# A Strassen-style GEGLU feed-forward kernel: two bf16 products moved ahead, one weight load in halves, the last output tile copied by two engines

## The chip, the cores and the metric

The kernel runs on one core of a Trainium2 chip. The metric is the device time of one execution in microseconds (us), the median of several runs. The engines of a core work side by side, each on its own queue in order: TensorE (PE; its weight loads are shown as PEld), VectorE (DVE), ScalarE (ACT), GpSimd (POOL) and SyncE (SP), which issues most of the DMAs here. They wait for one another through semaphores.

## The reference

```python
def setup_inputs():
    B, S, D, F = 32, 32, 1024, 3584
    return {
        "x": _w((lambda *s: _rng.normal(s) * 0.05)(B, S, D)),
        "w_gate": _w((lambda *s: _rng.normal(s) * 0.05)(D, F)),
        "w_up": _w((lambda *s: _rng.normal(s) * 0.05)(D, F)),
        "w_down": _w((lambda *s: _rng.normal(s) * 0.05)(F, D)),
    }

def reference(x, w_gate, w_up, w_down):
    return (_gelu(x @ w_gate) * (x @ w_up)) @ w_down
```

All tensors are bf16, gelu is the tanh form. x has 1024 rows (32 x 32) of 1024.

## The kernel before

Both matrix stages are done with seven block products instead of eight (the Winograd form of Strassen's scheme). Stage 1 treats [w_gate; w_up], cut along D, as a 2 by 2 block matrix for each block i of 128 columns of F (28 blocks, FT): A11 and A12 are the two halves of w_gate along D, A21 and A22 those of w_up. x, transposed, is the other 2 by 2 matrix: B11 and B21 are its first 512 rows (xt0), B12 and B22 its last 512 rows (xt1). A product P1 to P7 of one block is four matmuls of 128x128 by 128x512 into one PSUM tile.

- P1 (`first_products`, A11 B11) and P2 (`second_products`, A12 B21, on top of P1) read the bf16 weights and bf16 x themselves: "the bf16 products". They need nothing but their weights. ACT copies P1 to e1 (L212) and takes the gelu of P1 + P2 (L219).
- P6 (`sixth_products`, S2 T2), P7 (`seventh_products`, S3 T3), P5 (`fifth_product`, S1 T1), P4 (`fourth_product`, C22 T4) and P3 (`third_product`, S4 B22) work on fp32r sums and are f32r matmuls. T1 to T4 are sums of the four quarters of x, made once by DVE (`t_sum`, L166). S1 to S4 are sums of weight blocks for each i, made by DVE or POOL (L175, L176, L180, L184); C22 and the fp32r copy of B22 are made by ACT (L187, L291).
- P6 starts from e1 in PSUM (`seed`, L225). ACT copies P6's result to e2 (L241) before P7 goes on top of it; ACT copies P7's result to e3 (L256), and DVE adds it to P5 (u, L258), before P4 goes on top of it. DVE multiplies P4's result by the gelu (L245) into gT. P3 goes on top of P5, DVE adds e2 (h, L263; one buffer), ACT takes the gelu (L265), DVE multiplies by u (L268) into gT.

The order is written out by hand (`manual_schedule`): each engine's instructions stand in the order of the Python code. First come ten warm-up matmuls, then P1 and P2 of blocks 0 to 9 alone (LEAD = 10), while x's second half and the weights arrive and DVE makes the sums. Then P5, P6, P7, P4 and P3 of blocks 0 and 1 are done together, with the bf16 products of blocks 10 and 11 in between: P1 of block 10 after P5, P1 of block 11 after P6, P2 of block 10 after P7. From block 2 on a loop does one block a turn: P6, P4 of the block before, P5, then (`ahead`, not in the turns of ALONE) P1 of block `done` and P2 of block `done` - 1, then P7 and P3 of the block before. `done` starts at 12, so P2 of block 11 stands in the turn of block 2, behind P1 of block 12. Block 2 has no block before it in this sense, so its turn has no P4 and no P3.

SP's queue issues the weights in the order written: x's first two quarters, w_gate's tiles 0 to 3 (256 columns each, some in two halves along D), half of w_up's first tile, gate tile 4, the transposing load of xt1 (L155), gate tile 5 (blocks 10 and 11; it lies in the part of gT that is written last), the other half of w_up's first tile, gate tile 6, and so on. Each waits for the landing of an earlier DMA that used its semaphore, eight of which take turns.

Stage 2 multiplies gT by w_down in the same manner (L394). The last product, for each of four tiles of 128 rows, adds fourteen f32r matmuls to X[t]; ACT copies the 128x512 result to bf16 (L506) and it is stored, the first three by SP's queue, the last by ACT's.

PSUM has four tiles with the tag p (X and some of P1 + P2) and four with q (Y, the rest of P1 + P2), used in turn.

Of the kernel before, what the change touches and what calls it, by code (L numbers as in the profile page):

```python
# [7 lines left out]
ACT = mybir.ActivationFunctionType  # L8
# [4 lines left out]
def kernel(  # L13
# [18 lines left out]
    nc = tc.nc  # L32
# [10 lines left out]
    DT = D // P  # L43
    KH = DT // 2
    FT = F // P
    NT = N // P
    DB = 512
# [3 lines left out]
    LEAD = 10  # L51
    ALONE = (4, 7, 10, 13, 16, 19, 22, 25)
    KF = FT // 2
    TT = NT // 2
# [28 lines left out]
    def load_gate(c, queue, lo=0, hi=DT):  # L83
        if c not in WG:
            WG[c] = gw.tile([P, DT, 2 * P], bf16, name="gw", tag="gw")
        queue.dma_start(
            out=WG[c][:, lo:hi, :], in_=wg_r[:, lo:hi, 2 * c * P : (2 * c + 2) * P]
        )

    def load_up(c, lo=0, hi=4):  # L90
        if c not in WU:
            WU[c] = uw.tile([P, DT, 4 * P], bf16, name="uw", tag="uw")
        nc.sync.dma_start(
            out=WU[c][:, :, lo * P : hi * P],
            in_=wu_r[:, :, (4 * c + lo) * P : (4 * c + hi) * P],
        )
# [4 lines left out]
    def a11(i):  # L101
        return block(WG, 2, i, 0)

    def a12(i):
        return block(WG, 2, i, 1)
# [18 lines left out]
    def psum_p(name):  # L124
        return psum.tile([P, NB], fp32, name=name, tag="p")

    def psum_q(name):
        return psum.tile([P, NB], fp32, name=name, tag="q")

    with tc.manual_schedule():  # L130
# [22 lines left out]
        load_gate(3, nc.sync, KH, DT)  # L153
        load_gate(4, nc.sync)
        nc.sync.dma_start_transpose(out=xt1, in_=xf[NB:N, :])  # L155
        load_gate(5, nc.sync)
        load_up(0, 2, 4)

        T = {}
# [13 lines left out]
        def early_sums(i, engine=nc.gpsimd):  # L173
            S1[i], S3[i] = weight_tile("s1"), weight_tile("s3")
            engine.tensor_tensor(S1[i], a21(i), a22(i), ALU.add)  # L175
            engine.tensor_tensor(S3[i], a11(i), a21(i), ALU.subtract)  # L176
# [14 lines left out]
        def pair_product(ps, lhs, rhs, first, cuts):  # L191
            for lo, hi in zip(cuts, cuts[1:]):
                for p, l in zip(ps, lhs):
                    for k in range(lo, hi):
                        nc.tensor.matmul(  # L195
                            p,
                            lhsT=l[:, k, :],
                            rhs=rhs[:, k, :],
                            start=(first and k == 0),
                            stop=(k == KH - 1),  # L200
                            skip_group_check=True,
                        )

        def first_products(*blocks, cuts=(0, KH)):
            for i in blocks:
                A[i] = psum_p("a") if 4 <= i < 8 else psum_q("a")
            pair_product([A[i] for i in blocks], [a11(i) for i in blocks], B11, True, cuts)
            for i in blocks:
                if i % 2 == 0:
                    pool, tag = (xpool, "e1") if i == LEAD - 2 else (ring, "ring")  # L210
                    E1[i // 2] = pool.tile([P, 2, NB], fp32, name="e1", tag=tag)
                nc.scalar.activation(E1[i // 2][:, i % 2, :], A[i], ACT.Copy)  # L212

        def second_products(*blocks, cuts=(0, KH)):
            pair_product([A[i] for i in blocks], [a12(i) for i in blocks], B21, False, cuts)
            for i in blocks:
                if i % 2 == 0:
                    GL[i // 2] = half.tile([P, 2, NB], bf16, name="gl0", tag="half")
                nc.scalar.activation(GL[i // 2][:, i % 2, :], A[i], ACT.Gelu_apprx_tanh)  # L219

        X, Y, E2, U1, G1 = {}, {}, {}, {}, {}
# [5 lines left out]
        done = LEAD + 2  # L227

        def ahead():
            nonlocal done  # L230
            if done < FT:
                first_products(done)
            second_products(done - 1)
            done += 1

        def sixth_products(*blocks):
            cuts = range(0, KH + 1, 2)
            pair_product([X[i] for i in blocks], [S2[i] for i in blocks], T["T2"], False, cuts)
            for i in blocks:
                E2[i] = epool.tile([P, NB], fp32, name="e2", tag="e2")  # L240
                nc.scalar.activation(E2[i], X[i], ACT.Copy)  # L241
# [9 lines left out]
        def seventh_products(*blocks):  # L251
            cuts = range(0, KH + 1, 2)
            pair_product([X[i] for i in blocks], [S3[i] for i in blocks], T["T3"], False, cuts)
            for i in blocks:
                e3 = epool.tile([P, NB], fp32, name="e3", tag="e3")
                nc.scalar.activation(e3, X[i], ACT.Copy)  # L256
                U1[i] = epool.tile([P, NB], bf16, name="u1", tag="u1")
                nc.vector.tensor_tensor(U1[i], Y[i], e3, ALU.add)  # L258
# [28 lines left out]
        copy_a22(0)  # L287
        second_products(8)
        second_products(9)
        for k in range(KH):  # L290
            nc.scalar.activation(T["B22"][:, k, :], B22[:, k, :], ACT.Copy)  # L291
        copy_a22(1)
# [2 lines left out]
        pair_product(  # L295
            [Y[0], Y[1]], [S1[0], S1[1]], T["T1"], True, range(KH + 1)
        )
        first_products(LEAD)
        sixth_products(0, 1)
        first_products(LEAD + 1)  # L300
        seventh_products(0, 1)
        second_products(LEAD)
        early_sums(2, nc.vector)
        second_sum(2)
        seed(2)
# [12 lines left out]
        for i in range(2, FT + 1):  # L318
# [16 lines left out]
            if here and i not in ALONE and done <= FT:  # L335
                ahead()
# [55 lines left out]
        def step(ps, lhs, rhs, j, t, first=False, last=False):  # L392
            for i in range(2):
                nc.tensor.matmul(  # L394
                    ps,
                    lhsT=lhs[:, i, t * P : (t + 1) * P],
                    rhs=rhs[:, i, :],
                    start=(first and j == 0 and i == 0),
                    stop=(last and j == JF - 1 and i == 1),
                    skip_group_check=True,  # L400
                )
# [9 lines left out]
        X = [psum.tile([P, DB], fp32, name="x", tag="p") for t in range(TT)]  # L411
# [90 lines left out]
        for t in range(TT):  # L502
            for j in range(JF):
                step(X[t], SC[j], TC[j], j, t, last=True)
            o_sb = opool.tile([P, DB], bf16, name="o_sb", tag="o")
            nc.scalar.activation(o_sb, X[t], ACT.Copy)  # L506
            queue = nc.sync if t < TT - 1 else nc.scalar
            queue.dma_start(out=of[(TT + t) * P : (TT + t + 1) * P, 0:DB], in_=o_sb)

# [29 lines left out]
```

## Time and profile before

| what | value |
| --- | --- |
| runs of the kernel | 276.03 us median of 3 (275.87 to 276.15) |
| profiled execution | 276.09 us, span 274.28 us (first to last instruction) |
| granted TensorE clock | 1.000 over the span |
| first real matmul, last matmul's end | 5.74 us, 270.97 us |
| PE busy | 268.9 us, 98% of the span |
| DVE, ACT, POOL busy | 188.6, 138.2, 87.2 us |
| DMA | 26.42 MB, mean 96 GB/s |
| matmul of 128x512: bf16, f32r (start to start in a chain) | 0.22 us, 0.23 us |

The span is what the instructions cover; the time of an execution has some 1.8 us around it. In the chain of waits a row is a piece of the chain that ended last: its start, its length, the engine and the line, how many instructions. In a timeline a row is one or more instructions of an engine in order of time, with their start, duration, line, operation, shape, and in brackets the idle time before them and what ended it. A matmul's duration there (0.38 to 0.39 us) overlaps the next one's.

### The profile page before, as it was taken

The numbers are of one execution on the slowest core, as the hardware profiler recorded it, in microseconds if no ns is written. First come the engines' busy times: TensorE is split into PE (matmuls) and PEld (weight loads), VectorE is DVE, ScalarE is ACT, GpSimd is POOL, SyncE is SP. The second block draws the span as 40 slices with busy tenths as digits, with TensorE's granted clock in tenths as the row PEclk, the third lists the DMA queues.
The fourth block names the chain that finished last, engine by engine and source line by source line (L and its number), as shares of the span: only waits on it lengthen the run. The fifth ranks groups of instructions, "written<-read, shape, count | busy, mean of one in ns | idle before, by whom it ended". The sixth has DMA issues, their size and how long they took to land.

```text
span 274.3 us, 3336 instructions
## 1 busy us (share of the span) xinstructions
PE 268.9 (98%) x1172; PEld 189.3 (69%) x1186; DVE 188.6 (69%) x226; ACT 138.2 (50%) x239; POOL 87.2 (32%) x81
## 2 busy tenths in 40 slices
PE   8999999999999999999999999999999999999995
PEld 2445667768777687776877768764447888888883
DVE  0068974866658666686666866769994999999900
ACT  2678565566556665566655666531100072860311
POOL 0000083845558455584555845600000000000000
PEclk9999999999999999999999999999999999999999
DMA  8999402153400034215360202459602000000221
GB/s 174 280 272 269 155 1 76 51 181 103 128 2 0 0 102 131 76 44 187 97 211 0 76 2 77 114 190 327 215 0 76 2 0 0 1 2 0 97 96 38
DMA packets 41008, 26.42 MB, mean 96 GB/s; under 512 B 9248, under 2 KB 40992, under 8 KB 40992
## 3 DMA queue, kind: packets, MB, share of 16 engines
q1 hardware_dynamic: 39248, 25.30, 31.8%
q10 hardware_dynamic: 1744, 0.92, 1.3%
q8 instruction: 9, 0.15, 0.2%
q14 instruction: 7, 0.06, 0.1%
HBM read 22.02 MB, written 2.10 MB: 88 GB/s over the span
## 4 chain that ended last, share of the span: by engine, by line
PE 96%; DMA 2%; issue 0%; ACT 0%
PE x L195 19%; PE x L394 18%; PE y L115 18%; PE a L195 18%; PE x L115 9%; PE y L394 9%; PE z L394 4%; DMA xt<-in_x_dram 2%; PE y L195 1%; ACT o_sb L506 0%
## 5 line engine op out<-in xcount | busy, mean ns | idle before, releaser
L195 PE MATMUL x<-T,s 128*128 128x512 f32 x224 | 63.4, 407 | 0.0
L195 PEld LDWEIGHTS x<-T,s 128*128 128x128 f32 x224 | 41.6, 188 | 10.9 <-ACT e L241 0.3
L195 PE MATMUL a<-xt,gw 128*128 128x512 bf16 x182 | 44.0, 380 | 1.1 <-DMA xt<-in_x_dram 0.5
L184 POOL TENSOR_TENSOR s<-gw,s 128x512 fp32r<-128x512 bf16 x22 | 26.0, 1184 | 48.4 <-PE y L115 47.7
L258 DVE TENSOR_TENSOR u<-y,e 128x512 bf16<-128x512 f32 x28 | 19.3, 691 | 32.0 <-ACT e L256 31.2
L180 DVE TENSOR_TENSOR s<-s,gw 128x512 fp32r<-128x512 f32 x24 | 34.4, 1434 | 0.0
L195 PEld LDWEIGHTS <-gw 128*128 128x128 bf16 x192 | 17.4, 98 | 24.4 <-issue 5.7
L265 ACT ACTIVATE gl<-h 128x512 bf16<-128x512 bf16 x28 | 17.7, 631 | 28.5 <-DVE h L263 28.5
L245 DVE TENSOR_TENSOR gT<-gl,x 128x512 bf16<-128x512 bf16 x28 | 19.2, 687 | 17.9 <-PE x L115 17.9
L115 PE MATMUL x<-T,c 128*128 128x512 f32 x112 | 30.4, 393 | 0.0
L115 PE MATMUL y<-B,s 128*128 128x512 f32 x112 | 30.2, 391 | 0.0
L175 POOL TENSOR_TENSOR s<-uw 128x512 fp32r<-128x512 bf16 x25 | 29.2, 1167 | 0.0
L115 PE MATMUL y<-T,s 128*128 128x512 f32 x104 | 27.8, 389 | 0.0
L394 PE MATMUL x<-tc,sc 128*128 128x512 f32 x112 | 25.7, 389 | 0.0
L212 ACT ACTIVATE e<-a 128x512 f32<-128x512 f32 x28 | 16.6, 597 | 17.2 <-PE a L195 17.2
L256 ACT ACTIVATE e<-x 128x512 f32<-128x512 f32 x28 | 16.7, 600 | 15.7 <-PE x L195 15.7
L176 POOL TENSOR_TENSOR s<-gw,uw 128x512 fp32r<-128x512 bf16 x21 | 24.5, 1166 | 0.0
L115 PEld LDWEIGHTS x<-T,c 128*128 128x128 f32 x112 | 20.9, 188 | 5.1 <-ACT e L256 0.7
L115 PEld LDWEIGHTS y<-B,s 128*128 128x128 f32 x112 | 21.0, 188 | 4.7
L394 PEld LDWEIGHTS x<-tc,sc 128*128 128x128 f32 x112 | 21.0, 188 | 4.4
L115 PEld LDWEIGHTS y<-T,s 128*128 128x128 f32 x104 | 19.5, 188 | 4.1
L394 PEld LDWEIGHTS <-gT 128*128 128x128 bf16 x112 | 10.9, 98 | 13.3 <-issue 0.3
(57 smaller groups left out, 346.9 us busy)
## 6 DMA issues: line engine op xcount, KB each, us to landing
uw<-in_w_up_dram SPq DMA_DIRECT2D x6, 1024.0 KB, 6.3
gw<-in_w_gate_dram SPq DMA_DIRECT2D x8, 512.0 KB, 3.9
v<-in_w_down_dram SPq DMA_DIRECT2D x5, 512.0 KB, 3.5
v<-in_w_down_dram SPq DMA_DIRECT2D x4, 640.0 KB, 8.2
v<-in_w_down_dram SPq DMA_DIRECT2D x8, 256.0 KB, 4.2
out_dram<-o_sb SPq DMA_DIRECT2D x15, 128.0 KB, 1.7
gw<-in_w_gate_dram SPq DMA_DIRECT2D x5, 256.0 KB, 3.9
uw<-in_w_up_dram SPq DMA_DIRECT2D x2, 512.0 KB, 5.7
```

The source lines that it names most:

```text
L115: nc.tensor.matmul(ps, lhsT=lhs[:, k, :], rhs=rhs[:, k, :], start=(first and k == 0), stop=(k == KH - 1), skip_group_check=True,)
L175: engine.tensor_tensor(S1[i], a21(i), a22(i), ALU.add)
L176: engine.tensor_tensor(S3[i], a11(i), a21(i), ALU.subtract)
L180: nc.vector.tensor_tensor(S2[i], S1[i], a11(i), ALU.subtract)
L184: engine.tensor_tensor(S4[i], a12(i), S2[i], ALU.subtract)
L195: nc.tensor.matmul(p, lhsT=l[:, k, :], rhs=rhs[:, k, :], start=(first and k == 0), stop=(k == KH - 1), skip_group_check=True,)
L212: nc.scalar.activation(E1[i // 2][:, i % 2, :], A[i], ACT.Copy)
L245: nc.vector.tensor_tensor(gT[:, i, 0:NB], GL[i // 2][:, i % 2, :], X[i], ALU.mult)
L256: nc.scalar.activation(e3, X[i], ACT.Copy)
L258: nc.vector.tensor_tensor(U1[i], Y[i], e3, ALU.add)
L265: nc.scalar.activation(G1[i], h1, ACT.Gelu_apprx_tanh)
L394: nc.tensor.matmul(ps, lhsT=lhs[:, i, t * P : (t + 1) * P], rhs=rhs[:, i, :], start=(first and j == 0 and i == 0), stop=(last and j == JF ...
```

## The change

In stage 1, P1 of block 10 goes in front of P5 of blocks 0 and 1 (on ACT, its copy to e1 in front of the copies of B22). P1 of block 11 takes its old place after P5, P2 of block 10 stands after P6, and P2 of block 11 after P7, in front of P4 of block 0; the loop's first `ahead` (turn of block 2) then does P1 of block 12 alone. w_gate's sixth tile (number 5, blocks 10 and 11) is loaded in two halves along D, so that P1 waits for the first half alone: one more DMA on SP's queue. At the end, ACT copies the left 256 columns of the last output tile and DVE the right 256.

```diff
-        load_gate(5, nc.sync)
+        load_gate(5, nc.sync, 0, KH)
+        load_gate(5, nc.sync, KH, DT)
         load_up(0, 2, 4)
...
             nonlocal done
             if done < FT:
                 first_products(done)
-            second_products(done - 1)
+            if done > LEAD + 2:
+                second_products(done - 1)
             done += 1
...
         second_products(8)
         second_products(9)
+        first_products(LEAD)
         for k in range(KH):
             nc.scalar.activation(T["B22"][:, k, :], B22[:, k, :], ACT.Copy)
         copy_a22(1)
...
         pair_product(
             [Y[0], Y[1]], [S1[0], S1[1]], T["T1"], True, range(KH + 1)
         )
-        first_products(LEAD)
+        first_products(LEAD + 1)
         sixth_products(0, 1)
-        first_products(LEAD + 1)
+        second_products(LEAD)
         seventh_products(0, 1)
-        second_products(LEAD)
+        second_products(LEAD + 1)
         early_sums(2, nc.vector)
...
             o_sb = opool.tile([P, DB], bf16, name="o_sb", tag="o")
-            nc.scalar.activation(o_sb, X[t], ACT.Copy)
+            part = DB if t < TT - 1 else DB // 2
+            nc.scalar.activation(o_sb[:, :part], X[t][:, :part], ACT.Copy)
+            if part < DB:
+                nc.vector.tensor_copy(o_sb[:, part:], X[t][:, part:])
```

## The prediction

> **What bounds the kernel now.** I read the page's busy shares first, then the chain of work that ended last inside the stretch that the change touches, then the timelines of ScalarE (ACT) and VectorE (DVE) there, the DMA view of the moved load, and the timeline of the end. TensorE (PE) is busy for nearly the whole span, so only PE's gaps and the two ends can give time.
>
> ```profile
> PE 268.9 (98%) x1172; PEld 189.3 (69%) x1186; DVE 188.6 (69%) x226; ACT 138.2 (50%) x239; POOL 87.2 (32%) x81
> ```
>
> The chain between 22 and 46 us (start, length, what; counted at the ends of the matmuls):
>
> ```profile
> 23.34 2.12 PE y L195 x8
> 25.45 0.23 PE a L195
> 25.69 0.05 issue
> 25.74 0.59 PE a L195 x2
> 26.34 1.85 PE x L195 x8
> 28.19 0.88 PE a L195 x4
> 29.07 1.85 PE x L195 x8
> 30.92 0.88 PE a L195 x4
> 31.80 0.93 PE x L115 x4
> ...
> 39.02 1.86 PE x L195 x8
> 40.89 0.01 issue
> 40.90 1.19 PE x L115 x4
> ```
>
> Eight f32r matmuls take 1.85 us (0.92 for one product of four), four bf16 ones 0.87 to 0.88. P5 of blocks 0 and 1 (first line) takes 2.12: it waits 0.27 for T1, which DVE makes piece by piece. P4 of block 2 (last line) takes 1.19: it waits 0.27 for ACT's copy of P7's result. So some 0.55 us of PE time is lost in this stretch; after 43 us the chain shows f32r products of 0.91 to 0.93 and no gap worth having.
>
> ACT and then DVE between 30 and 38 us:
>
> ```profile
> 30.49 1.08 ACT L256 ACTIVATE e<-x 128x512 f32<-128x512 f32 x2 [0.78 <-PE x L195]
> 35.72 0.63 ACT L265 ACTIVATE gl<-h 128x512 bf16<-128x512 bf16 x1 [2.79 <-DVE h L263]
> 37.11 0.63 ACT L265 ACTIVATE gl<-h 128x512 bf16<-128x512 bf16 x1 [0.76 <-DVE h L263]
> 37.64 0.61 ACT L187 ACTIVATE c<-uw 128x512 fp32r<-128x512 bf16 x1
> 38.16 0.58 ACT L241 ACTIVATE e<-x 128x512 f32<-128x512 f32 x1
> ```
>
> ```profile
> 29.13 2.35 DVE L166 TENSOR_TENSOR T<-xt,T 128x1024 fp32r<-128x1024 bf16 x2
> 31.40 0.68 DVE L258 TENSOR_TENSOR u<-y,e 128x512 bf16<-128x512 f32 x1
> ```
>
> A second chain runs beside PE. DVE ends T4, does u, u, the three sums of block 2, gT, h with no idle time (h of block 0 starts at 35.00), ACT's gelu follows h at 35.72, h of block 1 needs that gelu's end (one h buffer), ACT does the second gelu, the copy L187 and at 38.16 e2 of block 2, and only its end (38.74) lets P7 of block 2 start at 38.79 (P7 and the next P6 take 1.86 instead of 1.85). So this second chain has no slack against PE. It starts at DVE's u of block 0 (31.40), which T4 holds now; e3, its other input, was ready at 30.49 + 0.60 = 31.09.
>
> **The change, part by part.** PE does the same matmuls; only the order moves.
>
> *1. P1 of block 10 in front of P5.* It needs the first half of w_gate's sixth tile. The DMA view from 20.1 to 24.1 us, in slices of 0.1 us:
>
> ```profile
> GB/s 289 292 287 292 292 289 289 292 292 289 289 289 289 279 129 56 72 56 31 108 195 261 307 307 297 317 287 348 338 364 343 348 338 358 343 333 348 338 364 317
> ...
> gT<-in_w_gate_dram SPq DMA_DIRECT2D x1, 512.0 KB, 4.4
> ```
>
> SP issues the load at 20.10, right behind the transpose of x (its issue holds SP's queue from 13.38 to 20.05), and it lands 4.4 us later, 24.47. The transpose's packets fill the rate until about 21.5; summing the slices from there, 262 KB have passed at 22.85 and 524 KB at 23.61. The whole tile's landing came 0.86 after its last bytes. If the half pays that lag in full it lands at 23.71; if half of it, at 23.28; I take 23.6, near the full lag, since that is the one lag measured here. PE is free for P1 at 23.34 (matmul ends), which needs a landing by 23.13: from the landing to the end of four bf16 matmuls is 0.04 (the first landing of x, 0.74 + 4.96 = 5.70, to the first matmul at 5.74) plus 1.05 (25.30 to 26.34 now). So P1 ends at 23.6 + 1.09 = 24.69 instead of a free 24.21, PE waits 0.48, and P5, with T1 whole by then, ends at 26.54. Before, both were done at 26.34. ACT now has block 10's e1 copy in front of the four copies of B22 (from 23.87 now) and waits there until P1's end; they end some 1.4 later, near 27.4, and P3 of block 0 reads them after 33. Bounds: a landing by 23.13 makes this part 0.28 better than before, one at 23.75 some 0.35 worse.
> The Trainium skill, "DMA: Bandwidth & Descriptors", in the section Anatomy of one DMA, says that most of a DMA's fixed cost is the receipt of the last write, so it does not shrink with the size; by that rule the half pays the whole lag and part 2 would come to +0.61, by half a lag to +0.18. The 0.86 us here is such a lag.
>
> *The split's other cost* is one more issue on SP: 0.56 us (four of 256 KB in a row took 2.23 from 7.74), so the second half, block 0's up half and the next gate tile start about 0.5 later. Their covers: P2 of block 10 reads the second half near 29.3 us, DVE's S1 of block 2 the up half after 32, P1 of block 12 the gate tile (21.43 + 7.6 = 29.0 now) after 37. So it costs nothing, and 0.5 us at most without that cover. Later loads keep their distance in the queue.
>
> *2. P2 of block 10 in front of P7, P2 of block 11 in front of P4.* By PE alone: 26.54, P1 of block 11 (0.87), P6 (1.85), P2 of block 10 (0.87), so P7 starts at 30.13, against 29.07. That is 1.06 later, and T2, T3, T4 are ready at each step. But e3 of block 0 now ends at 31.09 + 1.06 = 32.15 and DVE's u starts at 32.19 instead of 31.40, 0.79 later. PE's own work in front of P4 (P2 of block 11) does not help u, it only follows P7. Everything down the second chain is back to back or waits for the step before it, so e2 of block 2 ends 0.79 later as well and P7 of block 2 starts at 38.79 + 0.79 = 39.58, while PE is done with what stands before it at 39.20: 30.13 + 1.85 for P7 + 0.87 for P2 of block 11 = 32.85, plus 3.67 for the P4 and P3 of two blocks, 1.81 for P6 and P5 of block 2, 0.87 for P1 of block 12 (P2 of block 11 has left this place). From that start P7 and the next P6 take 2.10 (38.79 to 40.89), so P4 of block 2 can start at 41.68 instead of 39.20 + 1.85 = 41.05. Behind u on DVE stand the sums of block 2, then on POOL those of block 3: S2 of block 2 ends near 35.3 for P6 at 36.5, S2 of block 3 (37.32 + 1.66 now) near 39.8 for P6 at 40.8. ACT, rid of the gelu L219 between, has e3 at 40.76 + 0.60 + 0.04 = 41.40, so the old 0.27 wait goes. Before, P4 ended at 42.09, so its free start would be 42.09 - 0.92 = 41.17: **+0.51**. In general it is landing minus 23.09, with a floor of +0.04 when the half comes in time: the gap at P5 and the one at P4 are both closed, and the sum reappears in front of P7. Behind it the chain is all PE, and I carry +0.51 to the end.
>
> *3. The last tile by two engines.* Timeline of the end:
>
> ```profile
> 271.00 0.60 ACT L506 ACTIVATE o_sb<-x 128x512 bf16<-128x512 f32 x1 [2.58 <-PE x L394]
> 271.62 0.37 ACTq L508 DMA_DIRECT2D out_dram<-o_sb  x1
> ```
>
> In the built order the DVE half does not wait for PE but for ACT's counter at the value that ACT's half raises: the halves follow each other. ACT's half: 0.60 for 512 columns less 256 of them at 0.84 ns ((1052 - 620) / 512, lines L484 and L291) = 0.38. DVE's half has no row; the nearest is DVE's sum from PSUM of 512 columns, 0.69 (L408), less 256 at 1.04 ns ((1219 - 687) / 512, L166) = 0.42; the low bound is half of the fastest DVE row of 512 columns (0.41, L268) = 0.20. With 0.03 for the step between engines: 0.38 + 0.03 + 0.42 - 0.60 = **+0.23** (from +0.01). The store then waits for DVE instead of ACT, at the same price.
> The Trainium skill, "PSUM — Partial Sum Buffer", section PSUM bank collisions raise a hardware error, says that two engines may not access one bank at the same time, and that the compiler's scheduler orders such pairs, ACT and DVE reads too. A row of 512 fp32 is one bank of 2 KiB by that page, and the built order agrees. By the rule +0.23; with both halves at once 0.42 - 0.60 = -0.18.
>
> **Sum**: 0.51 + 0.23 = +0.74. The profiled execution (276.09 us, span 274.28) would become 276.83, its span 275.02; from the median of the runs, 276.03, it is **276.8**.
>
> **Rivals.** *Cover without a price*: the half lands by 23.13 and something on the second chain gives way (DVE does the sums of block 2 before u, or e2 is not what holds P7), so PE runs free: P1 and P5 end at 23.34 + 0.87 + 1.85 = 26.06, 0.28 sooner than now, P7 of block 2 starts at 39.02 - 0.28 = 38.74 and P4 at 40.59, 0.58 better than 41.17. With the tail's +0.23 it is 275.7. For it: both old gaps lie where the products go. Against: P7's wait at 38.79 already ends with L241, and u cannot precede e3. It decides if e2 ends before 38.7. If the tail's halves also ran together (-0.18): 275.3, faster.
> *The half in time, the chain as I read it*: +0.04 + 0.23 = 276.3. For it: rates up to 364 GB/s in the second half of the transfer. Against: the 0.86 lag.
> *A late half*: packets of both halves mixed, or the lag grown, landing at 24.1: +1.0 + 0.23 = 277.3. For it: three loads wait behind the transpose. Against: the whole tile landed before the load issued after it.
> *The halves together* with the rest as forecast: +0.51 - 0.18 = 276.36. Against: the counter that DVE waits for.
>
> **How the numbers follow.** Forecast 0.52; half in time 0.18; late half 0.13; cover without a price 0.09 (a third of it with the tail together); halves together 0.08. A measurement here tells some 0.2% (0.55 us) from no change. The forecast's own spread is 0.18 to 0.61 for the moves and 0.01 to 0.23 for the tail, so about a sixth of it (0.08) stays under 0.55. Slower: the rest of the forecast and the late half, 0.57; faster: the third of the free case, 0.03; within 0.2%: 0.40. Forecast alone: 276.4 to 277.0. The range 275.9 to 277.2 leaves out half of the late case and the free case, 0.16.
>
> **What would show it.** The chain has P5 at about 1.85, some 0.5 us of DMA wait ahead of the first P1 matmul on the tile in gT, and P7 of block 2 released by L241 near 39.6, with P4 of block 2 back at 0.92; u of block 0 at 32.2 behind ACT's e3. At the end ACT's half (0.38) and then DVE's (0.42), not side by side. P7 of block 2 starting before 39, or DVE's copy starting with ACT's, makes it wrong.

## The result

The changed kernel takes 276.80 us (median of 11 runs, 276.50 to 277.13) against 276.14 us for the kernel before beside it (11 runs, 275.87 to 276.61). The ratio is 1.0024, with a 95% interval from 1.0016 to 1.0032: slower by 0.66 us, 0.44 to 0.88. The profiled execution took 277.12 us with a span of 275.33 us, and the clock was granted in full.

PE is as busy as before in share:

```profile
PE 269.2 (98%) x1172; PEld 189.7 (69%) x1186; DVE 189.2 (69%) x227; ACT 138.3 (50%) x239; POOL 87.2 (32%) x81
```

The chain of waits between 20 and 48 us (start, length, what; several rows left out) answers to the first one shown of before:

```profile
25.01 1.82 PE y L196 x8
...
30.46 1.40 PE x L196 x6
31.85 0.02 issue
31.88 0.61 ACT e L258
32.48 0.02 issue
32.51 0.52 DVE u L260
...
36.20 0.61 DVE h L265
...
36.83 0.64 ACT gl L267
...
37.50 0.70 DVE h L265
...
38.76 0.61 ACT c L188
39.38 0.49 ACT e L243
39.87 0.04 issue
39.91 2.11 PE x L196 x8
42.02 0.97 PE x L115 x4
```

Before, this chain ran on PE alone. Now it leaves PE at P7 of blocks 0 and 1 (30.46), goes by ACT's e3 and DVE's u, through DVE's sums, h, ACT's gelu, the second h, the copy of A22 and e2, and comes back to PE at 39.91. P5 (first row) takes 1.82 us and has no wait for T1 any more, P4 of block 2 (last row) takes 0.97 instead of 1.19. The old gap at P5 is closed, 0.05 us is left of the one at P4, and a new one stands in front of P7 of block 2.

The waits between 20 and 46 us (who waited, for whom: us in total, times, longest):

```profile
PEld x L196 <- ACT e L243: 0.9, 1, 0.9
...
PEld L196 <- DMA gT<-in_w_gate_dram: 0.5, 1, 0.5
PE x L196 <- ACT e L243: 0.4, 1, 0.4
```

The weight load for P7 of block 2 stood idle for 0.9 us until e2 was copied; before, that wait was 0.3. The first weights of P1 of block 10 waited 0.5 us for the half tile (PE's matmuls only some 0.15, see below). It landed 3.7 us after its issue at 20.27, that is at 23.93.

At the end of the timeline the two halves of the last tile follow each other:

```profile
271.89 0.38 ACT L510 ACTIVATE o_sb<-x 128x256 bf16<-128x256 f32 x1 [2.58 <-PE x L397]
272.31 0.42 DVE L512 CAST o_sb<-x 128x256 bf16<-128x256 f32 x1 [11.02 <-ACT o_sb L510]
272.76 0.36 ACTq L514 DMA_DIRECT2D out_dram<-o_sb  x1
```

DVE starts when ACT has ended, and the store's issue comes 0.87 us after the start of ACT's copy instead of 0.62: +0.25.

### The profile page after: what moved, and what is told of

It is laid out like the page before. It is cut to its first block, busy times and chain, and to the rows that moved or that the text cites. A ratio compares the mean times of both kernels' runs of the same rounds, so it can differ in the third digit from the quotient of the medians.

```text
span 275.3 us, 3341 instructions
## 1 busy us (share of the span) xinstructions
PE 269.2 (98%) x1172; PEld 189.7 (69%) x1186; DVE 189.2 (69%) x227; ACT 138.3 (50%) x239; POOL 87.2 (32%) x81
## 4 chain that ended last, share of the span: by engine, by line
PE 93%; DVE 2%; DMA 1%; ACT 1%; SPq 1%; issue 1%; ACTq 0%
PE x L196 18%; PE x L397 18%; PE y L115 17%; PE a L196 15%; PE y L397 9%; PE x L115 9%; PE z L397 4%; PE warm L139 1%; DMA gw<-in_w_gate_dram 1%; SPq L148 1%; PE y L196 1%; DVE h L265 0%; DVE u L260 0%; ACT gl L267 0%; ACT c L188 0%
## 5 line engine op out<-in xcount | busy, mean ns | idle before, releaser
L220 ACT ACTIVATE gl<-a 128x512 bf16<-128x512 f32 x28 | 16.7, 597 | 6.7 <-PE a L196 6.6
```

## The experiments

The first four ran on one chip beside 27 runs of the kernel before (median 276.32 us), the last three on another beside 27 more (median 276.36 us). The differences in us are the recorded ratio times this median; this ratio is not that of the two medians (in experiment 7 the medians differ by 0.34 us, where the ratio gives 0.11). A profile is one execution of its kernel.

**1. The tail alone.**

```diff
-            nc.scalar.activation(o_sb, X[t], ACT.Copy)
+            part = DB if t < TT - 1 else DB // 2
+            nc.scalar.activation(o_sb[:, :part], X[t][:, :part], ACT.Copy)
+            if part < DB:
+                nc.vector.tensor_copy(o_sb[:, part:], X[t][:, part:])
```

> The kernel before with the last tile copied by two engines and nothing else. If ACT's half and DVE's half follow each other: +0.23 us on the kernel before (0.38 + 0.03 + 0.42 instead of 0.60), with DVE's copy starting some 0.03 behind ACT's end. If they run together: -0.18, both starting with the last matmul's end.

276.58 us, ratio 1.0011 (1.0001 to 1.0021): +0.30 us, 0.03 to 0.58. The timeline of its end:

```profile
271.25 0.38 ACT L507 ACTIVATE o_sb<-x 128x256 bf16<-128x256 f32 x1 [2.58 <-PE x L394]
271.66 0.42 DVE L509 CAST o_sb<-x 128x256 bf16<-128x256 f32 x1 [10.20 <-ACT o_sb L507]
```

DVE waits 0.03 behind ACT's end, and ACT's start to the store's issue (272.12) is 0.87 us again. The halves are serial; the -0.18 of the other theory is out.

**2. The moves alone.** The changed kernel with these lines instead of the two halves:

```diff
-            part = DB if t < TT - 1 else DB // 2
-            nc.scalar.activation(o_sb[:, :part], X[t][:, :part], ACT.Copy)
-            if part < DB:
-                nc.vector.tensor_copy(o_sb[:, part:], X[t][:, part:])
+            nc.scalar.activation(o_sb, X[t], ACT.Copy)
```

> The changed kernel with the last tile copied by ACT alone. The chain theory: +0.4 to +0.6 us on the kernel before (the landing of the half less 23.09), P4 of block 2 without its wait, P7 of block 2 released by ACT's e2. Rival, that the loss is the tail alone and the moves are free: 0.0.

276.75 us, ratio 1.0014 (1.0006 to 1.0023): +0.39 us, 0.17 to 0.63. The moves are not free, and the two parts add up, well within their intervals: 0.30 + 0.39 = 0.69 for 0.66. In its chain the half lands at 23.97, and P4 of block 2 ends at 43.02 (42.99 in the changed kernel, landing 23.93), again with the old wait all but gone.

**3. ACT's copy of A22 of block 2 out of the way.** To the changed kernel:

```diff
         for i in range(2):
             fourth_product(i)
+            if i == 0:
+                copy_a22(2)
             third_product(i)
-        copy_a22(2)
```

> The changed kernel with ACT's copy of A22 of block 2 taken out of the way: it stands behind P4 of block 0 instead of between the second gelu and e2 of block 2. The chain theory: e2 of block 2 and P7 of block 2 come 0.5 us sooner, so 0.5 us less than the changed kernel, +0.2 on the kernel before. Rival, that the loss is PE's wait for the half tile and nothing behind it: no difference from the changed kernel.

276.72 us, ratio 1.0012 (1.0003 to 1.0021): +0.33 us on the kernel before, where the changed kernel has +0.66. Its chain between 22 and 46 us:

```profile
25.06 1.83 PE y L196 x8
...
38.78 0.81 PE a L196 x3
39.59 1.96 PE x L196 x8
41.55 0.96 PE x L115 x4
```

The chain stays on PE the whole way. P5 begins as late as in the changed kernel (25.06 and 25.01), and still P4 of block 2 ends at 42.51 instead of 42.99: one ACT copy of 0.61 us, taken off the second chain, gives back 0.48 us. So the wait for the half tile is not by itself the loss. The times agree in sign (0.33 less), but do not settle it alone: the intervals, 0.08 to 0.58 here and 0.44 to 0.88 for the changed kernel, overlap. What shows the second chain is the trace.

**4. The gate tile whole.** To the changed kernel:

```diff
-        load_gate(5, nc.sync, 0, KH)
-        load_gate(5, nc.sync, KH, DT)
+        load_gate(5, nc.sync)
```

> The changed kernel with the sixth gate tile loaded whole. P1 of block 10 then waits for a landing some 0.8 us later. The chain theory: all of this comes through, +0.8 on the changed kernel, +1.4 to +1.6 on the kernel before. Rival, that the second chain has slack which takes the wait in, or that the halves land together: no difference from the changed kernel.

278.38 us (5 runs, 277.93 to 278.75), ratio 1.0073 (1.0061 to 1.0086): +2.02 us, 1.69 to 2.38. The profiled execution, at 278.02 near the low end, has this chain:

```profile
20.23 4.49 DMA gT<-in_w_gate_dram
24.72 0.05 issue
24.77 1.04 PE a L195 x4
25.80 1.85 PE y L195 x8
...
40.72 2.12 PE x L195 x8
42.84 0.96 PE x L115 x4
```

The tile lands at 24.72 instead of 23.93, 0.79 later, and P4 of block 2 ends at 43.80, 0.81 later than in the changed kernel: the whole delay comes through, and the halves do land apart. The median is some 0.4 us above the +1.6 expected; the profiled execution does not show it, and what the other four runs had was not traced, so that part stays open.

**5. P2 of block 11 alone.** To the kernel before:

```diff
-            second_products(done - 1)
+            if done > LEAD + 2:
+                second_products(done - 1)
...
         second_products(LEAD)
+        second_products(LEAD + 1)
         early_sums(2, nc.vector)
```

> The kernel before with P2 of block 11 alone moved, from the turn of block 2 to in front of P4 of block 0. The chain theory: P7 of blocks 0 and 1 is not touched, so DVE's u and everything behind it stay; ACT loses the gelu that stood in front of e3 of block 2, and P4 of block 2 loses its 0.27 us of waiting: -0.27 us on the kernel before. Rival, that putting a bf16 product in front of P4 delays what follows, as in the changed kernel: +0.2 to +0.5.

276.09 us, ratio 0.9992 (0.9983 to 1.0001): -0.22 us, -0.47 to +0.03. The rival's loss is excluded. The gain of 0.27 fits, but the interval just includes zero. Its chain:

```profile
23.79 1.85 PE y L195 x8
...
38.32 0.88 PE a L195 x4
39.20 1.94 PE x L195 x8
41.13 0.97 PE x L115 x4
```

P4 of block 2 takes 0.97: its wait is all but gone, though 0.09 us has come up in front of P7 (1.94 instead of 1.85). P5 takes 1.85, but not by the edit: PE itself came to P5 0.45 later than in the profile of before (23.79 against 23.34) and found T1 ready.

**6. P1 of block 10 alone.** To the kernel before, with the tile in halves:

```diff
         second_products(9)
+        first_products(LEAD)
...
             [Y[0], Y[1]], [S1[0], S1[1]], T["T1"], True, range(KH + 1)
         )
-        first_products(LEAD)
```

> The kernel before with P1 of block 10 alone in front of P5 and the gate tile in halves; P1 of block 11 and the P2 stay where they were. The chain theory: P1 waits for its half and P7 of blocks 0 and 1 comes 0.2 us later, which T4 still covers, so u stays and the rest is held by ACT's e3 of block 2 as before: 0.0 to +0.2 us. Rival, that the wait for the half is the loss of the changed kernel by itself: +0.4 to +0.5.

276.16 us, ratio 0.9996 (0.9987 to 1.0005): -0.11 us, -0.36 to +0.14. PE's timeline between 9 and 24 us, and rows of its chain:

```profile
20.28 4.05 PE L196 MATMUL a<-xt,gT 128*128 128x512 bf16 x18
```

```profile
24.76 1.85 PE y L196 x8
...
29.32 1.86 PE x L196 x8
...
41.13 1.13 PE x L115 x4
```

P5 starts at 24.76, but not late by the half: the matmuls on the tiles in gT run from 20.28 into P1 without a stop. PE itself came there 0.56 later than in the profile of before (20.28 against 19.72), and the half had landed by then (its weights are loaded from 23.72). P7 of blocks 0 and 1 starts 0.25 later than before (29.32), DVE's u starts right behind T4 (31.57), and P4 of block 2 has its old wait, a row of 1.13. So the late P1 is taken in, and by the times the +0.4 of the rival is excluded: P1 in front of P5 costs nothing that can be seen, as long as the second chain does not start later. The second DMA issue of the split is in this run too, and shows no price. What a wait for the half costs by itself is not shown here, since this profile has none.

**7. P1 of block 10 inside P5.** All moves, the copy early as in 3, the old tail:

```diff
-        first_products(LEAD)
...
-        pair_product(
-            [Y[0], Y[1]], [S1[0], S1[1]], T["T1"], True, range(KH + 1)
-        )
-        first_products(LEAD + 1)
+        for ks in (range(0, 3), range(2, KH + 1)):
+            pair_product([Y[0], Y[1]], [S1[0], S1[1]], T["T1"], True, ks)
+            first_products(LEAD + ks[0] // 2)
```

> All moves, but P1 of block 10 stands between the second and the third step of P5 (when its half has landed), ACT's copy of A22 of block 2 is early as in e3, and ACT alone copies the last tile. The chain theory: no wait at P5, P1, P7 or P4 of block 2 is left, or less than 0.1 us each: -0.3 to -0.6 us on the kernel before. Rival, that some other wait takes their place: 0.0 or more.

276.02 us, ratio 0.9996 (0.9986 to 1.0005): -0.11 us, -0.39 to +0.14. It is faster than the changed kernel (0.44 to 0.88), but part of that is the old tail; beside experiment 2, which has the same tail, the intervals only just do not meet (0.14 and 0.17). It is not resolved from the kernel before; the two medians differ by 0.34 us. Its chain:

```profile
23.40 1.26 PE y L196 x4
24.66 0.88 PE a L196 x4
25.54 0.93 PE y L196 x4
...
39.16 1.97 PE x L196 x8
41.13 0.96 PE x L115 x4
```

P1 (24.66) starts without a wait for its half, P5's second part and P4 of block 2 wait no more, and P7 of block 2 has 0.1 us left. The first part of P5 (1.26 for four matmuls, 0.92 when free) still waits for T1, some 0.3 us: here PE was early and x late. So not every wait went under 0.1, and the expected -0.3 was not shown.

## Why the prediction was right

The forecast was 276.8 us, +0.74 in two parts; measured are 276.80 and +0.66, and by the parts alone +0.39 and +0.30 against +0.51 and +0.23. That the total comes out to 0.03 us is luck: the moves were forecast too high, the tail too low, and the forecast started from 276.03, 0.11 below the runs beside the changed kernel. The mechanism is another matter, and was right in the step that decided; PE's own arrival was not.

- *The landing of the half.* I took 23.6 from a lag of the whole tile; it was 23.93 in the profile of after and 23.97 in experiment 2. In these executions x's second half landed later as well: DVE began T1 at 22.37 and 22.56, against 22.17 before. Counted from there the half came 1.56 and 1.41 later, where the forecast had 1.43. So most of the 0.33 us belongs to the execution and not to the split. The lag of a load behind its last bytes, by the prediction's way of counting, is an estimate: with the bytes summed from the end of the transpose, 262 KB have passed at some 22.95 in the profile of after and 22.9 in experiment 6, where the half landed at 23.93 and 23.68. That is some 1.0 and 0.8 us for the half beside 0.86 for the whole tile, so by this count the half paid the lag in full. The section that the prediction names for this in the Trainium skill, Anatomy of one DMA on the page "DMA: Bandwidth & Descriptors", describes DMAs that GpSimd issues; these are SP's.
- *PE's wait for it.* Forecast 0.48; this is where the working was off. In the profile of after it was only some 0.15, because PE itself came to P1 0.66 us later than in the profile of before (its first matmul on the tiles in gT is at 20.38 against 19.72): it had waited for a gate tile at 11.7 (below). In experiments 2, 3 and 6 that matmul is at 20.34, 20.50 and 20.28. If the prediction's free end of P1, 24.21, is moved by as much, P1 would have ended at 24.87, 24.83, 24.99 and 24.77 without any wait for the half; it ended at 25.01, 25.05, 25.06 and 24.76. So by this estimate the half held PE for 0.2 us at most, and a half landing in time would have gained these executions no more than that, where the sum has 0.47 (0.51 to 0.04). It was luck that the landing still came last in the profile of after, with P1's end 1.08 behind it (25.01) as the sum had it, and experiment 4 shows that a later landing comes through in full.
- *The second chain.* This was the step that decided, and it went as worked out from P1's end on. u at 32.51 (forecast 32.19), P7 of block 2 released at 39.91 (39.58): later by 0.32 and 0.33, the landing's 0.33. The order of the steps is that of the chain shown above. Experiment 3 shortens this chain and its trace has 0.48 us back (its times 0.33, not resolved); experiments 5 and 6 move a product without lengthening it and lose nothing that can be seen.
- *P4 of block 2.* Forecast free of waiting; it took 0.97, so 0.05 us of waiting for e3 are left. The rule "landing minus 23.09" gives 0.84 for a landing at 23.93; with these 0.05 it is 0.89, and the end of PE's work moved by 0.90 us between the two profiles (270.97 to 271.87). Part of this is x's later landing, 0.20, so some 0.7 in this execution is the moves; over the runs of experiment 2 it is 0.39 (0.17 to 0.63), against a forecast of 0.51.
- *The tail.* Forecast +0.23, 0.38 and 0.42 for the halves; measured 0.38 and 0.42, +0.25 from ACT's start to the issue, +0.30 (0.03 to 0.58) by time. That the two reads are ordered, which the Trainium skill's page "PSUM — Partial Sum Buffer" gives as a rule for one bank (section PSUM bank collisions raise a hardware error), is what the built order has and the trace shows; whether the chip would have let them run together was not tried.
- *The rivals.* Cover without a price needed e2 before 38.7; it ended at 39.87. The half in time had +0.04 for the moves; experiment 2 is above that. The late half was near 24.1. The landing, at 23.93 and 23.97, was in fact nearer to that than to 23.6, though mostly because x was late too; its price, +1.0 for the moves, lies outside the interval of experiment 2. The halves together would have made the tail 0.18 faster; experiment 1 has it slower.

## What to carry to other kernels

A gap that is filled on the busiest engine is only gained if no chain on the other engines is tied to the work that the filling pushes back: look for the chain that has no slack at the point where PE comes back to it, and count from the input that starts it. A move that puts work behind the start of such a chain (P2 of block 11, experiment 5) showed no cost; one product more in front of it (P2 of block 10, in the changed kernel) delays all of it. No run moved that product by itself. And a forecast from one profile takes over the accidents of that execution: here PE's early arrival, which only one of the eight other profiles shares. Sharing a copy between two engines shortens it only when the halves do not wait for each other, and that can be read from the built order.

## What was not expected of the hardware

The first 12 us differ between executions by more than most edits here. PE's wait for the first half of w_gate's fourth tile was 0.42 us in the profile of after and 0.38, 0.84, 1.25, 0.67, 0.99 and 0.77 in experiments 1 to 6; in the profiles of before and of experiment 7 no such wait is listed for the matmuls. The timeline of experiment 3 between 9 and 24 us, a late one:

```profile
11.85 8.81 PE L196 MATMUL a<-xt,gw 128*128 128x512 bf16 x39 [1.25 <-DMA gw<-in_w_gate_dram]
```

When PE is late here, the wait for T1 at P5 shrinks or goes (experiment 5), so part of it is taken in. x's landing differs too (T1 began between 22.17 and 22.57 in the profiles). The kernel before spread over 275.79 to 277.31 us within 27 runs; that these two make up the spread is not shown, since only single executions have a trace. Two profiles alone, 1.05 us of span apart, would have overstated the change by 0.4 us.
